# Gate and up of tokens 512 to 1023: from full products to seven block products with 256-token halves

## The chip, the cores and the metric

The kernel runs on one core of a Trainium2 chip. The metric is the device time of one execution in microseconds (us). The engines of a core work side by side, each through its own queue in order: TensorE (PE) multiplies matrices, VectorE (DVE), ScalarE (ACT) and GpSimd (POOL) do the elementwise work, SyncE (SP) issues the DMAs. PE writes its results into PSUM, from where VectorE and ScalarE take them.

## The reference

```python
x = A_x                                   # 1 x 2048 x 512, bfloat16
xn = layernorm(x)
qkv = xn @ wqkv                           # 512 x 1536; 32 heads of 16
pq, pk = q @ w_phi[h], k @ w_phi[h]       # 16 x 16 for each head
phi_q = concat(softmax(pq), softmax(-pq)) # 32 features; phi_k alike
kv, z = phi_k^T v, sum_s phi_k            # for each head, over all tokens
attn = (phi_q kv) / (phi_q z + 1e-6)
h = (xn @ w_gate) * (xn @ w_up)           # 512 x 1792 each
out = x + attn @ wo + h @ w_down          # 1792 x 512
```

All inputs and the output are bfloat16.

## The kernel before

2048 tokens are sixteen tiles of 128, in four groups of four (`GT` = 4, 512 tokens, `TT`). All weights and all of x stay in SBUF. `w_phi` is folded into the weights of q and k on the chip (`W1q`, `W1k`; steps `fq`, `fk`).

The work is cut into named steps, each a small function in the dictionary `steps`. One written list, `ORDER`, says in which order they are issued, and with `/v`, `/g` or `/a` on which engine (VectorE, GpSimd, ScalarE). No scheduler changes that order: every engine executes its own instructions in the order of the list, and semaphores hold it where data or a buffer is not ready. A second table, `SLOTS`, says which buffer of a ring each tile takes ("s" are six PSUM banks, "f" two more in the pool `ps_f`, "x", "g", "vt" are SBUF rings). The loop at the end also keeps "turns": after a VectorE step whose operands all lie in SBUF (its name matches `both_in_sbuf`), the next GpSimd instruction of the list waits for it.

The steps, by name:

- `s`, `sc`, `a`, `xt`: layer norm of a tile (statistics, scale, normalised x, DMA transposition). The transposed x of tokens 0 to 1023 lies in `xnT` (bfloat16), that of 1024 to 2047 in `x16` (float16).
- `k` or `vk`, `vc`, `kx`, `ky`, `kr`, `ki`, `kp`, `kv`: v and k products, exponentials on ScalarE, sums and reciprocals on VectorE, product on GpSimd, then the `kv` sums. `q`, `qx` to `qp`, `qt` are the same for q, with a DMA transposition; `ab`, `de`, `rd`, `ot`, `oT` are the attention of a tile.
- `g`, `gc`, `u`, `h` (`unit_steps`): gate and up of one group for 128 hidden columns: four matmuls for gate, a copy to SBUF (`gate_copy`), four matmuls for up, and the product of both on VectorE (`hidden`). Units 0 to 13 are tokens 0 to 511, units 14 to 27 tokens 512 to 1023; `half` issues the matmuls, with 512 columns.
- `p1` to `p7`, `k1` to `k3`, `j2`, `j7`, `j3`, `d4`, `m` (`block_steps`): gate (even block) and up (odd block) of tokens 1024 to 2047 by seven block products instead of eight. Tokens, input channels and hidden columns are each cut into two halves; `z` (sums of tokens) and `t` (differences of weights, after `up` has scaled them by a power of two) make the operands. A product is two matmuls with 512 columns into one of three PSUM banks `sa`, `sb`, `sc`. Bank `sa` keeps a running sum: product 1, copy `k1`, product 6 on top, copy `k2`, product 7, copy `k3`, product 4, then `d4`. The joins `j` add a bank and a kept copy; `m` multiplies up by gate.
- `f` (`fin_steps`): down product and attention output of one tile; `fs` adds x, `fo` stores.
- `n`, `wr`, `wf`, `wp`, `ws`, `inv`: powers of two for the scaled weights. `S`, `cb`, `ct`, `wt` and the steps with capital `P`, `K`, `A`, `J`, `X` (`pair_steps`): seven block products for the down product of six pairs of tiles of tokens 1024 to 2047.
- `=k`, `=ab`, `=f`, `=ab2`: change the PSUM pool of the two banks besides the six.

## Time and profile before

| | |
|---|---|
| time, median of 3 runs | 214.32 us (214.11 to 214.84) |
| the profiled execution | 214.6 us, span of its instructions 212.8 us |
| PE, DVE, ACT, POOL busy | 207.8, 181.5, 138.2, 140.3 us |
| instructions of these | 1368 matmuls, 333, 247, 133 |
| granted TensorE clock, mean | 0.999 |
| moved by DMA | 19.91 MB |

The profile is one execution, taken by the hardware profiler. A row of a group reads: line of the kernel, engine, operation, what it writes and reads, form, number of instructions, then busy time in us, mean length of one in ns, and the idle time of the engine ahead of them with what ended it. A row of the chain gives the start, the length, and the work. L333 is the matmul in `half`, L319 the one in `proj` (k, v, q), L797 the one in `block_steps`, L663 that in `fin_steps`, L924 that in `pair_steps`; L353 is `hidden`, L339 to L345 are the branches of `copy`, L819 is `times` (the m steps), L758 the weight differences, L894 the hidden sums, L507 the transposition of x.

### The profile page before, as it was taken

How to read it: one execution, taken by the hardware profiler on the slowest of the kernel's cores; microseconds unless marked ns; L12 is line 12 of the kernel's file. 1: busy time of each engine (PE TensorE's matmuls, PEld its weight loads, DVE VectorE, ACT ScalarE, POOL GpSimd, SP SyncE). 2: the span in 40 equal slices, each digit the busy share in tenths (PEclk: the TensorE clock that was granted, in tenths of full speed). 3: DMA queues.
4: the chain of work that ended last, by engine and by line, in shares of the span. 5: the costliest groups of instructions: out<-in, count | busy, mean ns of one | idle time of the engine just before them, and what ended most of it. 6: DMA issues, size and time to landing. Idle time of an engine off the chain costs nothing.

```text
span 212.8 us, 3868 instructions
## 1 busy us (share of the span) xinstructions
PE 207.8 (98%) x1368; PEld 109.8 (52%) x1368; DVE 181.5 (85%) x333; ACT 138.2 (65%) x247; POOL 140.3 (66%) x133
## 2 busy tenths in 40 slices
PE   7999999999999999999999999999999999999993
PEld 3554444444454455554454444444444455678982
DVE  4857998986967889889878999999999999997853
ACT  4616999977756897889943966765487457254200
POOL 3600350776678898987887986567697888927370
PEclk9999999999999999999999999999999999999999
DMA  5999996050133002021545540020405506525342
GB/s 161 260 283 385 376 288 80 12 115 0 28 78 72 0 3 49 0 52 37 101 89 88 111 99 18 11 43 6 99 0 93 84 2 138 87 42 91 74 117 74
DMA packets 47250, 19.91 MB, mean 94 GB/s; under 512 B 37504, under 2 KB 46976, under 8 KB 47104
## 3 DMA queue, kind: packets, MB, share of 16 engines
q1 hardware_dynamic: 47232, 19.69, 41.2%
q8 instruction: 10, 0.16, 0.3%
q14 instruction: 8, 0.07, 0.1%
HBM read 8.67 MB, written 2.10 MB: 51 GB/s over the span
## 4 chain that ended last, share of the span: by engine, by line
PE 91%; DMA 3%; DVE 2%; SPq 1%; issue 1%; DVEq 0%
PE fin L663 16%; PE g L333 12%; PE u L333 11%; PE sa L797 11%; PE k L319 6%; PE pv L319 6%; PE q L319 6%; PE sc L797 5%; PE da L924 4%; PE sb L797 3%; PE kv L574 2%; DMA oT<-otok 2%; PE db L924 2%; PE dd L924 2%; PE dc L924 2%; PE ab L611 2%
## 5 line engine op out<-in xcount | busy, mean ns | idle before, releaser
L533 DVE TENSOR_REDUCE sums<-e 128x64 f32<-128x1024 f32 x32 | 38.4, 1204 | 3.5 <-ACT e L521 3.3
L543 POOL TENSOR_TENSOR phiq<-e,rs 128x1024 bf16<-128x1024 f32 x16 | 31.0, 1944 | 11.4 <-ACT dK L341 4.2
L663 PE MATMUL fin<-wd,hT 128*128 128x512 bf16 (+2 forms) x154 | 37.9, 360 | 0.0
L543 POOL TENSOR_TENSOR phik<-e,rs 128x1024 bf16<-128x1024 f32 x16 | 30.9, 1940 | 7.3 <-DVE rs L538 2.8
L333 PEld LDWEIGHTS <-wgu 128*128 128x128 bf16 x240 | 22.8, 98 | 23.4 <-DMA wgu<-in_B_w_gate_dram 0.3
L333 PE MATMUL u<-xnT,wgu 128*128 128x512 bf16 (+1 forms) x120 | 27.9, 365 | 0.0
L333 PE MATMUL g<-xnT,wgu 128*128 128x512 bf16 (+1 forms) x120 | 27.8, 365 | 0.0
L353 DVE TENSOR_TENSOR hT<-u,g_sb 128x512 bf16<-128x512 f32 (+1 forms) x30 | 18.8, 637 | 5.5 <-PE u L333 5.4
L663 PEld LDWEIGHTS <-hT 128*128 128x128 bf16 (+1 forms) x154 | 14.5, 98 | 14.8
L262 POOL TENSOR_SCALAR ve<-mv 128x1 f32<-128x1 f32 (+1 forms) x7 | 2.1, 293 | 24.9 <-DVE mv L258 24.8
L538 DVE RECIPROCAL rs<-sums 128x64 f32<-128x64 f32 x32 | 17.2, 542 | 1.2
L521 ACT ACTIVATE e<-k 128x512 f32<-128x512 f32 x24 | 13.3, 598 | 6.8 <-PE k L319 6.7
L521 ACT ACTIVATE e<-q 128x512 f32<-128x512 f32 x24 | 13.5, 601 | 6.4 <-PE q L319 6.3
L797 PEld LDWEIGHTS <-T 128*128 128x128 f16 x112 | 10.6, 98 | 11.9
L797 PE MATMUL sa<-ss,T 128*128 128x512 f16 x56 | 16.2, 379 | 0.0
L339 ACT CAST g_sb<-g 128x512 bf16<-128x512 f32 (+1 forms) x21 | 11.4, 568 | 7.1 <-PE g L333 6.5
L341 ACT ACTIVATE k<-sa 128x512 f32<-128x512 f32 x19 | 11.3, 602 | 6.1 <-PE sa L797 6.1
L339 ACT COPY k<-sa 128x512 f32<-128x512 f32 x19 | 11.2, 589 | 5.8 <-PE sa L797 4.8
L698 ACT ACTIVATE junk<-wgu 128x1024 bf16<-128x1024 bf16 x14 | 14.8, 1059 | 0.0
L319 PEld LDWEIGHTS <-xnT 128*128 128x128 bf16 x96 | 9.0, 98 | 10.7 <-ACT xnT L307 1.4
L758 POOL TENSOR_TENSOR T<-wgu,T 128x512 f16<-128x512 bf16 x9 | 10.6, 1176 | 5.8 <-DVE T L758 3.9
L319 PEld LDWEIGHTS <-x 128*128 128x128 f16 x96 | 9.0, 98 | 10.1 <-DVE otok L639 0.2
(153 smaller groups left out, 480.2 us busy)
## 6 DMA issues: line engine op xcount, KB each, us to landing
out_dram<-o_sb SPq DMA_DIRECT2D x15, 128.0 KB, 2.0
wd<-in_B_w_down_dram SPq DMA_DIRECT2D x1, 1792.0 KB, 16.1
wgu<-in_B_w_gate_dram SPq DMA_DIRECT2D x2, 640.0 KB, 7.2
wgu<-in_B_w_up_dram SPq DMA_DIRECT2D x2, 640.0 KB, 8.3
xall<-in_A_x_dram SPq DMA_DIRECT2D x1, 1024.0 KB, 12.4
xall<-in_A_x_dram SPq DMA_DIRECT2D x4, 128.0 KB, 2.6
vk<-in_A_wqkv_dram SPq DMA_DIRECT2D x2, 256.0 KB, 3.7
wgu<-in_B_w_gate_dram SPq DMA_DIRECT2D x2, 256.0 KB, 4.7
```

The lines of the kernel that those rows point to most:

```text
L319: nc.tensor.matmul(ps, lhsT=xt(n)[:, j, :], rhs=w[:, j, :], start=(j == 0), stop=(j == DC - 1))
L333: nc.tensor.matmul(ps, lhsT=w[:, c, f * P:(f + 1) * P], rhs=xnT[:, c, T * TT + lo:T * TT + hi], start=(c == 0), stop=(c == DC - 1))
L339: A.copy(out=dst, in_=src)
L353: V.tensor_tensor(out=hT(T)[:, f, lo:hi], in0=ps, in1=g_sb[:, 0:hi - lo], op=ALU.mult)
L521: A.activation(out=held[s + "e", n][:, :, sign, :], in_=held[s, n].rearrange("p (g c) -> p g c", g=NG), func=AF.Exp, scale=(nrst if sign e ...
L533: V.tensor_reduce(out=sums[:], in_=ev(), axis=AX.X, op=ALU.add)
L538: V.reciprocal(out=rs[:].rearrange("p a b -> p (a b)"), in_=held.pop((s + "s", n))[:])
L543: eng.tensor_tensor(out=phi[:].rearrange("p g (x f) -> p (g x) f", f=DH), in0=ev(), in1=held.pop((s + "i", n))[:].to_broadcast((P, 2 * H, ...
L663: nc.tensor.matmul(held["fin", n, lo], lhsT=l, rhs=r, start=len(done) == 1, stop=len(done) == FC + DC)
L698: A.activation(out=out, in_=cols, func=AF.Square, accum_out=nrm[:, g, k:k + 1])
L797: nc.tensor.matmul(mine[bankname], lhsT=ww[:, j, :], rhs=xx[:, j, :], start=start and j == 0, stop=(j == hc - 1), skip_group_check=True)
L924: nc.tensor.matmul(mine[ps][:, 0:W], lhsT=l, rhs=r, start=bool(mine.pop((ps, "new"), False)), stop=True, skip_group_check=True)
```

## The change

Units 14 to 27 are taken away. Tokens 512 to 1023 get block steps of their own, with an N ahead of the name (`Np1.0`, `Nk1.0`, `Nj2.0`, ...), with halves of 256 tokens: a product is two matmuls with 256 columns, and keeps, joins and m steps work on 256 columns. The weight differences `t` are shared with tokens 1024 to 2047. The transposed x of these tokens moves from `xnT` to a tile of its own, `x4`, in float16, with token sums `s4` beside it (steps `Nz`). Since their gate and up are now scaled, their h is float16, and their denominators and output use the scale of the block products (`scale_of`). The banks `sa` and `sc` of the new blocks come from the two banks of `ps_f`, `sb` from the six; q and f steps no longer use `ps_f`. The tile of `t2` (differences of down weights) moves to smaller pieces in the "vt" ring, and the up results from "vt" to "g". `inv` is cut in two steps. The list and the slots are written anew: 1244 words instead of 1072.

The core of the diff (the list and the slot table are cut to a few lines):

```diff
 ORDER = """
-g2 gc2/v u0 g3 gc3/a u2 h2 g1 u1 gc1/v h1 fk2 g0 gc0/v u3 fka2/a h3 h0 fk0 fkv0/v g8 g4 fkv2/a fka0/a k0 gc8/v
...
+g3 gc3/a =k g1 gc1/a fk2 fk0 g0 u3 fkv2/v fkv0/v fka2/a fka0/a k1 ky1 kx1 u0 gc0/v h3 k0 u1 k2 h0 kr1 h1 ki1 kx0
+ky0 kr0 s6 s5 ky2 n1.0 g4 g6 gc4/a u6 g7 n0.5 kx2 gc6/a gc7/a s7 k3 kp1/g s4 sc4 kx3 n1.6 n0.6 ky3 u7 h7 h6 a5/g
+xt5 u4 g12 g11 g13 h4 ki0 u12 g9 u13 a6/g kp0/g gc11/a s9 s11 s10 s8 u11 a4/a xt4 n0.3 gc9/a kr2 gc13/a n0.1 h11
+h13 xt6 wq g10 gc10/a gc12/a kr3 n2.4 u9 h9 ki2 kv0 g5 sc8 a11/g a10/g vk5.0 a8/g xt11 ki3 vk5.1 kp2/g a9/a
...
+Np2.1 ab7 de7/a f3.6 p5.1 f3.7 k3.1/a rd7 ot7 qy13 p4.1 p3.0 =f fs3 Np1.1 up31/a Nk1.1/a Np1.0 Nk1.0/a p2.3
+Np6.1 qx13 j3.0 Np6.0 p2.2 Nj2.1 Nk2.1/a j7.1 d4.1 Nk2.0/a up30/a t11/g m2.1/g Np2.0 Nj2.0 t12/g p3.1 j3.1 Np7.0
+Np7.1 Nk3.1/a Nk3.0/a p1.2 k1.2/a p1.3 qr9 m7.1/g Np4.1 Np4.0 Nd4.0/a p5.2 t13/v Np5.0 up40/a Nd4.1 p6.2 Nj7.0
...
-    xnT = npool.tile([P, DC, HALF], BF16, name="xnT", tag="xnT")
+    xnT = npool.tile([P, DC, TT], BF16, name="xnT", tag="xnT")
+    x4 = xpool.tile([P, DC, TT], F16)
+    s4 = xpool.tile([P, 4, DC // 2, TT // 2], F16)
...
-        return xnT[:, :, n * P:(n + 1) * P] if n < QT else x16[:, :, (n - QT) * P:(n - QT + 1) * P]
+        x, lo = (xnT, 0) if n < GT else (x4, GT) if n < QT else (x16, QT)
+        return x[:, :, (n - lo) * P:(n - lo + 1) * P]
...
-    for u in range(2 * FC):
+    for u in range(FC):
         unit_steps(u)
...
-        new_bank = bank_f if n in QF else bank
+        new_bank = bank
...
-    def block_steps(b):
+    def block_steps(b, group):
         k, g = b // 2, b % 2
         hc = DC // 2
+        n = TT // 2 if group else TT
+        tag = "N" if group else ""
         cols = pair_cols(k)[:, g]
+        A11, A12, A21, A22 = narrow if group else wide
...
         def h(t, i):
-            return hT(NGRP // 2 + t)[:, k + i * FH, :]
+            return hT(1)[:, k + i * FH, t * n:(t + 1) * n] if group else hT(NGRP // 2 + t)[:, k + i * FH, :]
...
                 if start:
-                    mine[bankname] = bank(bankname)
+                    new_bank = bank_f if group and bankname != "sb" else bank
+                    mine[bankname] = new_bank(bankname)[:, 0:n]
...
-                mine[name] = ring(xnpool, "x", [P, TT], F32, name)
+                mine[name] = ring(xnpool, "x", [P, n], F32, name)
                 copy(eng, mine[name][:], mine["sa"], gate_scale if g == 0 else None)
...
-                    mine["u", i] = ring(vpool, "vt", [P, TT], BF16, "u_sb")
+                    mine["u", i] = ring(gpool, "g", [P, n], BF16, "u_sb")
                     V.tensor_tensor(out=mine["u", i][:], in0=mine[ps], in1=mine[kept][:], op=ALU.add)
...
     for b in range(2 * FH):
-        block_steps(b)
+        block_steps(b, 0)
+        block_steps(b, 1)
...
+    SMALL = ((0, 2), (2, 4), (4, 6), (6, FH))
...
-    QF = (8, 9, 13, 10, 14)
```

## The prediction

> **What bounds the kernel now.** I read the page's first part, then the chain of work that ended last, then busy time by stretch, and last the groups by form.

> ```profile
> PE 207.8 (98%) x1368; PEld 109.8 (52%) x1368; DVE 181.5 (85%) x333; ACT 138.2 (65%) x247; POOL 140.3 (66%) x133
> PEclk9999999999999999999999999999999999999999
> PE 91%; DMA 3%; DVE 2%; SPq 1%; issue 1%; DVEq 0%
> ```

> TensorE (PE) is busy 98% of the span, and the chain that ended last lies on it for 91%. A busy PE need not be PE at its peak, so I look at its pace in the chain, listed in order of time:

> ```profile
> 9.73 0.44 PE u L333 x4
> 22.30 1.73 PE g L333 x8
> 24.89 1.73 PE u L333 x8
> 170.50 0.86 PE sc L797 x4
> 204.11 1.53 PE dc L924 x14
> 208.48 0.78 PE da L924 x7
> 209.28 0.48 DVE o_sb L953
> ```

> Eight matmuls with 512 columns take 1.73 us, four take 0.86: 0.216 us each, in bfloat16 (g, u) as in float16 (sc). Fourteen with 256 columns take 1.53 us: 0.109 each, and the bfloat16 ones at the start (u x4) 0.44, or 0.11. At full clock these are flat paces, so PE is fed almost without a gap. After its last product only one join (0.48 us) and the last store are left. PE's work is the time, unless another engine falls behind. How near the others are:

> ```profile
> 0.00:20.00 20.00, 18.59 (x132) 9.69 (x133) 13.14 (x35) 9.07 (x21) 5.92 (x21) 1.00 0.93 264
> 20.00:100.00 80.00, 80.00 (x517) 38.66 (x516) 69.04 (x113) 67.28 (x120) 54.82 (x43) 1.00 0.37 83
> 100.00:177.00 77.00, 77.00 (x424) 36.34 (x423) 71.75 (x129) 51.39 (x88) 59.94 (x48) 1.00 0.33 62
> 130.00:190.00 60.00, 59.95 (x348) 30.28 (x347) 57.99 (x103) 36.26 (x60) 44.15 (x38) 1.00 0.29 53
> ```

> After the stretch's length the columns are PE, weight load, VectorE (DVE), ScalarE (ACT), GpSimd (POOL). From 100 to 177 us, where block products run, DVE is busy 71.75 of 77.0 us (93%), and from 130 to 190 us 58.0 of 60 (97%), with PE still full. DVE is the one engine with little left.

> **The change part by part.** The rows that price it:

> ```profile
> L333 PE MATMUL g<-xnT,wgu 128*128 128x512 bf16 x104 | 25.6, 379 | 0.0
> L333 PE MATMUL u<-xnT,wgu 128*128 128x512 bf16 x104 | 25.5, 379 | 0.0
> L924 PEld LDWEIGHTS <-wgu 128*128 128x128 f16 x84 | 8.1, 98 | 1.6
> L353 DVE TENSOR_TENSOR hT<-u,g_sb 128x512 bf16<-128x512 f32 x26 | 17.2, 670 | 5.0 <-PE u L333 5.0
> L353 DVE TENSOR_TENSOR hT<-u,g_sb 128x256 bf16<-128x256 f32 x4 | 1.7, 422 | 0.5 <-PE u L333 0.4
> L343 DVE CAST g_sb<-g 128x512 bf16<-128x512 f32 x7 | 4.8, 680 | 2.6 <-PE g L333 2.6
> L343 DVE CAST vt<-pv 128x512 bf16<-128x512 f32 x4 | 2.7, 672 | 0.1
> L339 ACT CAST g_sb<-g 128x512 bf16<-128x512 f32 x19 | 10.6, 588 | 7.0 <-PE g L333 6.5 <-DVE hT L353 0.4
> L339 ACT CAST g_sb<-g 128x256 bf16<-128x256 f32 x2 | 0.7, 373 | 0.1
> L341 ACT ACTIVATE k<-sa 128x512 f32<-128x512 f32 x19 | 11.3, 602 | 6.1 <-PE sa L797 6.1
> L341 ACT ACTIVATE dK<-da,inv 128x256 f32<-128x256 f32 x7 | 3.3, 470 | 6.8 <-issue 4.0 <-PE da L924 2.7
> L819 POOL TENSOR_TENSOR hT<-u_sb,hT 128x512 f16<-128x512 bf16 x7 | 8.0, 1156 | 2.2 <-DVE hT L819 1.4 <-DVE down L727 0.8
> L819 DVE TENSOR_TENSOR hT<-u_sb,hT 128x512 f16<-128x512 bf16 x14 | 7.9, 585 | 0.0
> L894 DVE TENSOR_TENSOR wgu<-hT 128x384 f16<-128x384 f16 x5 | 1.6, 327 | 0.0
> L758 DVE TENSOR_TENSOR T<-wgu 128x512 f16<-128x512 bf16 x5 | 2.5, 493 | 0.0
> L341 ACT ACTIVATE wgu<-wgu,up 128x1024 bf16<-128x1024 bf16 x12 | 13.9, 1155 | 0.0
> ```

> *PE.* Units 14 to 27 go: 14 x 8 = 112 matmuls of 512 columns, 112 x 0.216 = 24.2 us. Fourteen blocks of seven products of two matmuls come: 196 of 256 columns, 196 x 0.109 = 21.4 us. The weight load of one takes 98 ns and fits under 109. Projections and down products keep their number. Saved on the path: 2.8 us, and nothing else of PE changes.

> *DVE.* Gone are 14 `hidden` products (0.670), 7 wide and 1 narrow gate casts, 4 v casts (these go to ACT) and two wide keeps (taken at the casts' 0.68): 9.4 + 4.8 + 0.4 + 2.7 + 1.4 = 18.7 us. New are 42 half joins and 7 half `direct` products; no such row exists before, and I take the 256-column row, 0.422, for it too reads PSUM and writes 16 bits: 49 x 0.422 = 20.7. The other moves: 9 half m steps at some 0.35 (an estimate, over half of 0.585) and 4 wide ones fewer, +0.8; five hidden sums more (0.327) 1.6; two weight differences (0.493) 1.0; two wide copies from PSUM (0.68) 1.4; in all +5, and the rest is smaller than a step or two. So DVE goes from 181.5 to about 188.5, all of it beside PE as long as it keeps up. [...]

> *ACT.* 41 half keeps (between 0.373 and 0.470; I take 0.42), 7 half directs, 4 more wide keeps (0.60), 4 v casts and 2 more weight scalings (1.155) come, 7 gate casts (0.588) go: about +20 us, to 158 of some 210 (75%). *POOL* gets 12 half m steps and 4 wide ones (1.156): some +8 us, to about 148. Both stay covered by PE's 205, but neither cover is loose: ACT's list is densest before 120 us, where before it was already busy 67.3 of 80 us.

> *Where the list is tight.* Between the first block product and the step `=ab2` the new list holds 98 + 25 + 12 pairs of wide matmuls (products, down, q), 98 pairs of half ones and 4 attention steps: 58.3 + 21.4 + 1.0 = 80.7 us of PE. The DVE steps between the same two points sum to 87.8 us of durations. The same count of the old list gives 77.8, and that stretch is the one from 100 to 177 us, busy 71.75: neighbours overlap, a factor 0.92. So 0.92 x 87.8 = 81 us of DVE meet 81 us of PE: 100%, where before it was 93%, and 97% was sustained for 60 us without loss. Behind `=ab2` DVE has room (35 us of durations under 39 of PE), so steps can slip some us. I put the loss at 0.4 us; its ends are 0 (the 97% row) and 3 us (DVE's old idle share of 4% stays).

> *The start.* The first v and k products of tokens 512 on move up. Old and new:

> ```profile
> 11.72 1.03 PE L333 MATMUL g<-xnT,wgu 128*128 128x512 bf16 x4
> 43.11 0.38 PE L319 MATMUL pv<-vk,xnT 128*128 128x512 bf16 x1
> 27.53 6.43 SPq L507 DMA_TRANSPOSE xnT<-xn  x4
> DMA to landing us min/median/max: 3.7/5.5/6.0
> wT<-in_A_wqkv_dram SPq DMA_TRANSPOSE x2, 5.0
> ```

> The list starts at 11.72 us; ahead of `vk5.0` it now has 22 wide groups of 0.864, four half ones of 0.436, two folds and a `kv` (some 1 us): 21.7 us, so PE is there at 33.4 us instead of 43.1. The first transposed x was issued at 27.5 and takes 3.7 to 6.0: it lands at 31 to 33.5, the next ones some 1.2 us apart. The wait lies between 0 and 2 us; I take 0.2, as the transposition is listed about a microsecond earlier. On SP's queue the transposition of the q weights (`wq`) moves up from sixth to fourth, behind the third x; issued near 30.7 us it lands near 36, and `fq0`, which reads it, comes at 37.7 us. The turns make the next POOL step wait for a DVE step that works in SBUF alone; five more of these m steps at 0.585 us or less make at most 3 us of POOL waiting, in an engine that is idle for a third of the span, with only later feature products queued behind: nothing on the path, and at most those 3 us if that cover were gone.

> Sum for the profiled execution (214.6 us, of which 212.8 are span): 214.6 - 2.8 + 0.4 + 0.2 = 212.4. The median of the runs lies 0.3 below that execution (214.3), so the prediction is 212.1.

> **The rivals.** *VectorE takes over in the product stage.* If the halves cost as much as the 256-column joins at the end of the chain (0.48 instead of 0.422), DVE asks for 84 us against 81, and some of its idle time stays: 1 to 2.5 us lost, 213.1 to 214.6. For it: the 100% above. Against: 97% without loss, and slack behind `=ab2`.

> *The hand-offs of the small bank (ends slower).* A half block keeps its running sum in one bank `sa`: product 1, copy by ACT, product 6, copy, product 7, copy, product 4. PE may not go on until the copy is done. Counting list steps, old blocks leave at least 1.3 us of other PE work between two such products, for a copy of 0.60; new half blocks leave as little as 0.65 (mostly 0.9 to 1.1) for a copy of 0.37 to 0.47, and the ACT queue may have a weight scaling of 1.155 us in front. There are 42 such hand-offs, each on PE's in-order queue; from 2.8 / 42 = 0.067 us each on the gain is gone. At 0.1 to 0.2 us each it costs 4.2 to 8.4 us: 215.7 to 219.9, middle 217.5. For it: the thin spacing and the denser ACT. Against: the old list has the same kind of hand-off 42 times, and PE's pace shows none.

> *Half-width matmuls are not half price.* If weight load and start cost kept one at 0.123 us (24.2 / 196) or more, the gain is gone; at 0.14 it is 196 x 0.031 = 6.1 us dearer, 218.2. [...] The chain's 0.216 and 0.109 speak plainly against it.

> **How the numbers follow.** The forecast (PE sets the time, up to 1 us lost; 211.4 to 212.9) gets 0.57. VectorE's takeover 0.22: 0.12 of it faster, 0.08 no change, 0.02 slower. Hand-offs 0.14, half-width price 0.03, both slower. An early start that waits its full 2 us and more 0.04, half faster and half no change. About 0.3% (0.64 us) is what the measurement can tell from no change. So faster 0.57 + 0.12 + 0.02 = 0.71, the same 0.08 + 0.02 = 0.10, slower 0.19. The range starts at 211.2 (no loss anywhere and the run spread of 0.2) and reaches to 216.0, where it takes in the takeover and the cheap end of the hand-offs; some 0.15 is left above.

> **What would show it.** Right: the new half products in the chain at 0.109 us, chain shares on PE of 90% or more, DVE near 188 and over 95% in the product stage, ACT near 158, the first v product near 33.5 us, and the last join near 207.1. Wrong: gaps of PE ahead of `sa` that ACT's keep ends (hand-offs), PE waiting for banks that a DVE join frees (takeover), a wait of the first v product for the transposition, or a half product above 0.11 us.

## The result, and the profile after

The changed kernel takes 214.12 us (median of 22 runs, 212.70 to 215.21), the kernel before, measured beside it, 214.80 us (22 runs, 214.11 to 215.63). The ratio is 0.9968, 95% interval 0.9952 to 0.9983: faster by 0.7 us. Forecast were 2.2 us less. The profiled execution took 215.05 us, 0.9 more than the median, so its waits are probably larger than those of a usual execution.

The page's first part, granted clock and chain of the changed kernel:

```profile
PE 206.5 (97%) x1452; PEld 117.8 (55%) x1452; DVE 185.3 (87%) x372; ACT 153.2 (72%) x296; POOL 149.8 (70%) x146
PEclk9999999999999999999999999999999999999999
PE 78%; DMA 9%; DVE 6%; SPq 2%; ACT 1%; POOL 1%; issue 1%; DVEq 0%; ACTq 0%; POOLq 0%
```

PE held 91% of the chain before and holds 78% now; DMA came to 9%, VectorE to 6%. So the time is no longer PE's work alone. The stretches (columns as in the prediction: length, then PE, weight load, DVE, ACT, POOL) say where:

```profile
20.00:100.00 80.00, 77.59 (x549) 37.76 (x548) 72.75 (x125) 73.83 (x136) 65.43 (x51) 1.00 0.55 117
100.00:177.00 77.00, 76.96 (x471) 44.48 (x470) 72.29 (x158) 55.20 (x115) 59.31 (x58) 1.00 0.16 28
130.00:190.00 60.00, 60.00 (x398) 34.76 (x396) 54.41 (x120) 33.72 (x68) 42.37 (x39) 1.00 0.29 59
```

From 100 to 190 us, where the new half products run, PE is full (76.96 of 77, 60.00 of 60). All that is lost lies between 20 and 100 us: 80.00 - 77.59 = 2.4 us idle, where before there was none. PE's rows in order of time show five waits in it:

```profile
33.60 0.38 PE L337 MATMUL pv<-vk,x 128*128 128x512 bf16 x1
38.34 0.41 PE L471 MATMUL pq<-bd,wT 64*128 64x64 bf16 x16 [0.26 <-DMA wT<-in_A_wqkv_dram]
43.51 0.39 PE L337 MATMUL pv<-vk,x 128*128 128x512 bf16 x1 [0.85 <-DMA x<-xn]
72.54 0.43 PE L590 MATMUL kv<-vt,phik 128*128 128x68 bf16 x8 [0.39 <-POOL phik L559]
74.43 0.43 PE L590 MATMUL kv<-vt,phik 128*128 128x68 bf16 x8 [0.17 <-POOL phik L559]
94.24 0.61 PE L678 MATMUL fin<-wo,oT 128*128 128x512 bf16 x2 [0.72 <-DMA oT<-otok]
```

The brackets sum to 2.39 us, all of the 2.41. (By starts it is 3.2 us: each first matmul also starts late by what the modelled end of its neighbour covers, 0.16 us.) (L337, L590, L627, L678 and L824 are the matmuls of `proj`, `kv`, `ab`, `fin_steps` and `block_steps` in the changed file, L960 that of `pair_steps`, L471 that of the folds.) In steps these are `fq0` at 38.34, `vk7` at 43.51, `kv14` and `kv15`, and `f3.8`. The first v product, at 33.60, did not wait. What each waited for, out of the chain of waits:

```profile
31.84 6.46 DMA wT<-in_A_wqkv_dram
40.98 2.47 DMA x<-xn
66.50 2.10 DVE ss L796
72.15 2.23 POOL phik L559 x2
89.45 4.74 DMA oT<-otok
```

and SP's queue in order of time:

```profile
31.84 2.92 SPq L491 DMA_TRANSPOSE wT<-in_A_wqkv_dram  x1
34.85 7.36 SPq L523 DMA_TRANSPOSE x<-xn  x5
```

The q weights took 6.46 us to land; the x of `vk7` was issued only at 40.98, fifth in a row on SP's queue; VectorE's token sum `z0` (line 796) took 2.10 us, which made GpSimd's phik late; the transposed attention output of tile 3 landed after 4.74 us.

### The profile page after: what moved, and what is told of

It reads as the page before. It is cut to its first block, busy times and chain, and to the rows that moved or that the text cites. A ratio compares the mean times of both kernels' runs of the same rounds, so it can differ in the third digit from the quotient of the medians.

```text
span 213.3 us, 4174 instructions
## 1 busy us (share of the span) xinstructions
PE 206.5 (97%) x1452; PEld 117.8 (55%) x1452; DVE 185.3 (87%) x372; ACT 153.2 (72%) x296; POOL 149.8 (70%) x146
## 4 chain that ended last, share of the span: by engine, by line
PE 78%; DMA 9%; DVE 6%; SPq 2%; ACT 1%; POOL 1%; issue 1%; DVEq 0%; ACTq 0%; POOLq 0%
PE sa L824 16%; PE fin L678 15%; PE sc L824 9%; PE k L337 5%; PE q L337 5%; PE da L960 5%; PE pv L337 4%; PE sb L824 4%; DMA wT<-in_A_wqkv_dram 3%; PE u L351 3%; DMA wgu<-in_B_w_up_dram 2%; PE g L351 2%; DMA oT<-otok 2%; PE db L960 2%; PE dd L960 2%; PE dc L960 2%
## 5 line engine op out<-in xcount | busy, mean ns | idle before, releaser
L678 PE MATMUL fin<-wd,hT 128*128 128x512 bf16 (+2 forms) x154 | 37.1, 359 | 0.0
L559 POOL TENSOR_TENSOR phiq<-e,rs 128x1024 bf16<-128x1024 f32 x16 | 31.5, 1975 | 4.8 <-DVE hT L846 2.7
L824 PEld LDWEIGHTS <-T 128*128 128x128 f16 x224 | 21.9, 98 | 17.4 <-issue 0.5
L846 POOL TENSOR_TENSOR hT<-u_sb,hT 128x256 f16<-128x256 bf16 (+1 forms) x23 | 21.1, 920 | 5.3 <-DVE T L774 3.0
L357 ACT COPY k<-sa 128x512 f32<-128x512 f32 (+1 forms) x42 | 19.5, 483 | 5.6 <-PE sa L824 4.1
L359 ACT ACTIVATE k<-sa 128x512 f32<-128x512 f32 (+1 forms) x41 | 19.7, 494 | 4.9 <-PE sa L824 4.2
L824 PEld LDWEIGHTS <-wgu 128*128 128x128 bf16 x168 | 16.3, 98 | 12.3
L337 PEld LDWEIGHTS <-x 128*128 128x128 f16 x144 | 13.4, 98 | 14.4 <-DMA x<-xn 1.1
L678 PEld LDWEIGHTS <-hT 128*128 128x128 f16 (+1 forms) x154 | 14.0, 98 | 11.8
L337 PE MATMUL pv<-vk,x 128*128 128x512 bf16 x48 | 18.2, 379 | 0.8 <-DMA x<-xn 0.8
L337 PE MATMUL k<-vk,x 128*128 128x512 bf16 x48 | 18.2, 379 | 0.0
L824 PE MATMUL sa<-ss,T 128*128 128x512 f16 x56 | 16.3, 379 | 0.0
L839 DVE SCALAR_TENSOR_TENSOR hT<-sc,k 128x512 f16<-128x512 f32 (+1 forms) x28 | 15.3, 548 | 1.1 <-PE sc L824 0.9
L359 ACT ACTIVATE wgu<-wgu,up 128x1024 bf16<-128x1024 bf16 x14 | 16.0, 1152 | 0.0
L843 DVE TENSOR_TENSOR u_sb<-sc,k 128x512 bf16<-128x512 f32 (+1 forms) x28 | 15.0, 545 | 0.6 <-PE sc L824 0.5
L537 ACT ACTIVATE e<-q 128x512 f32<-128x512 f32 x24 | 13.9, 601 | 1.9 <-POOL phik L559 1.4
L351 PE MATMUL u<-xnT,wgu 128*128 128x512 bf16 (+1 forms) x64 | 14.6, 352 | 0.1
```

The source lines that it names most:

```text
L337: nc.tensor.matmul(ps, lhsT=xt(n)[:, j, :], rhs=w[:, j, :], start=(j == 0), stop=(j == DC - 1))
L351: nc.tensor.matmul(ps, lhsT=w[:, c, f * P:(f + 1) * P], rhs=xnT[:, c, lo:hi], start=(c == 0), stop=(c == DC - 1))
L357: A.copy(out=dst, in_=src)
L359: A.activation(out=dst, in_=src, func=AF.Identity, scale=scale)
L559: eng.tensor_tensor(out=phi[:].rearrange("p g (x f) -> p (g x) f", f=DH), in0=ev(), in1=held.pop((s + "i", n))[:].to_broadcast((P, 2 * H, ...
L678: nc.tensor.matmul(held["fin", n, lo], lhsT=l, rhs=r, start=len(done) == 1, stop=len(done) == FC + DC)
```

## Experiments

Theory at this point: PE's own saving came, and was given back in these five waits, which have three causes: the start, the sum z0 (one of the token sums `z`, VectorE's row at 66.50), and the late transposition of tile 3 (oT3). The rival: VectorE or GpSimd is short of time from 20 to 100 us in any order, so that a wait taken away comes back at the next step. Each ratio below is to the kernel before.

**The start and the sum z0, each alone.** Both edits move words of the list and nothing else. The first:

```diff
-... vk6.0 s14 fq0 xt10 s15 s12 sc12 xt8 xt9 xt7 ky4 kx4 ky5 fqa0/v vk6.1 ky6 kv1 g2 ...
+... vk6.0 s14 xt7 xt10 s15 s12 sc12 xt8 xt9 ky4 kx4 ky5 vk6.1 ky6 kv1 fq0 fqa0/v g2 ...
```

> The changed kernel with two steps moved in its list: the transposition of x of token tile 7 (xt7) is issued ahead of those of tiles 10, 8 and 9, and the fold of the q weights (fq0) comes after the next v and k products and a kv step, 1.1 us later on PE. Waits theory (the new waits of PE in the first half gave the gain back): the waits of 0.43 us ahead of fq0 and 1.0 us ahead of vk7 go, the time falls by 1.0 to 1.4 us against the changed kernel, ratio to the kernel before 0.990 to 0.993. Backlog theory (VectorE and ScalarE are so full that a wait taken away here comes back later): under 0.4 us, ratio 0.995 to 0.998. Chance theory (the waits of the profiled execution were its own): about half, 0.5 to 0.8 us, ratio 0.993 to 0.995.

Measured: 213.82 us, ratio to before 0.9938 [0.9915, 0.9961]. The waits at `fq0` and `vk7` are gone, the others stand (0.39 us at `kv14`, 0.69 us at `f3.8`). The second:

```diff
-... kp12/g kp13/g z0/v n0.2 kx14 ... kvm0 kvm1 =ab ...
+... kp12/g kp13/g n0.2 kx14 ... kvm0 kvm1 z0/v =ab ...
```

> The changed kernel with one VectorE step moved: the token sum z0, which took 2.10 us while GpSimd worked (0.90 in the kernel before), is issued after kvm1 instead of ahead of the features of tiles 14 and 15. Waits theory: the features are ready 2 us earlier, the waits of 0.56 and 0.33 us ahead of kv14 and kv15 go, the time falls by 0.7 to 1.0 us, ratio 0.992 to 0.994. Backlog theory: the 2.1 us of VectorE stay in its queue and delay the next joins or attention steps instead; under 0.3 us, ratio 0.996 to 0.999. If z0 takes 0.9 us at its new place, its length was due to what GpSimd did beside it; if it takes 2.1 again, it is slow wherever GpSimd runs.

Measured: 213.54 us, 0.9934 [0.9912, 0.9956]. At its new place z0 took 0.82 us. `kv14` and `kv15` no longer wait; `vk7` still does (0.88 us), and a new wait stands at 97 us (0.74 us, an attention product for a transposed phiq). Two causes, then, worth 0.6 and 0.7 us of the median by the middles of the intervals (0.9968 to 0.9938 and to 0.9934). Each interval still overlaps that of the change a little; and `fq0` and `f3.8` did not wait in the second profile, which its edit does not explain.

**The last wait, and all three.** `f3.8` is moved from behind `oT3` to just ahead of `f3.6`, some 4 us later; then all three moves together:

```diff
-... k3.0/a oT3 f3.8 fs0 rd6 ... ab7 de7/a f3.6 ...
+... k3.0/a oT3 fs0 rd6 ... ab7 de7/a f3.8 f3.6 ...
```

> The changed kernel with one PE step moved: the down product's attention part f3.8, which was listed right behind the transposition of its operand oT3 and waited 0.88 us for it, comes some 6 us of PE work later. Waits theory: 0.5 to 0.9 us less, ratio 0.993 to 0.995. Backlog theory: PE's products then stand 0.9 us earlier against the joins, and PE waits there instead; under 0.3 us, ratio 0.996 to 0.998. Chance theory: the transposition took 4.7 us in that one execution against a usual 2.5, so 0.0 to 0.3 us on the median, too.

> The three edits together (xt7 and fq0, z0, f3.8). Waits theory: 2.5 to 3.2 us less than the changed kernel, so the whole saving of 2.8 us on PE against the kernel before shows, ratio 0.983 to 0.988, and PE waits for nothing longer than 0.3 us between 15 and 205 us. Backlog theory: VectorE, at 185 of 213 us before, would have to be busy some 98% from 60 to 177 us, and PE waits for its joins; under 1 us less, ratio 0.992 to 0.997. Hand-off theory (PE waits for ScalarE's copies of the small bank once it runs ahead): waits of 0.1 us or more at many of the 42 half hand-offs, ratio 0.990 to 0.995.

Measured: alone 214.71 us, 0.9988 [0.9967, 1.0008], no gain; all three 212.97 us, 0.9905 [0.9889, 0.9922], short of the 0.983 to 0.988 expected. The wait for oT3 only went to the next in line: with `f3.8` moved alone the attention product behind it waits 0.43 us for VectorE's otok (the attention output before its transposition). That profile also shows how much the waits change between executions: its start is that of the change, yet `fq0` does not wait and `vk7` only 0.20 us. PE with all three moves:

```profile
75.36 1.02 PE L337 MATMUL q<-W1q,x 128*128 128x512 bf16 x4 [0.20 <-DVE fro L728]
93.28 0.41 PE L627 MATMUL ab<-KV,phiqT 128*128 128x68 bf16 x8 [1.28 <-DVE otok L654]
```

The attention product at 93.28 waits for VectorE's otok, which waits for a buffer that oT3 still reads: its transposition took 4.59 us, from 87.76 to 92.35. Moving the reader does not help while the transposition is late. Start and z0 without the third move:

> The change with two of the three moves at once: the transposition xt7 ahead of its four neighbours and the first product of the fq0 group behind kv1, and the VectorE sum z0 behind kvm1. Waits theory: the two savings of the single runs add, about 0.65 and 0.75 us of the median behind the change itself, so a ratio near 0.990 against the kernel before (about 212.7 us), unless the attention chain of tiles 4 to 7 takes some of it back with a wait of 0.5 to 1.5 us near 90 to 97 us (then 0.992). Rival, that the single gains were chance of the chip or one and the same slack: ratio 0.9935, no better than either alone. Against the run of all three moves (0.9905) it says what moving f3.8 is worth on top: nothing, if its wait only goes to the next in line.

Measured: 212.67 us, 0.9892 [0.9872, 0.9913]. The two add, the third move shows no gain on top, and the late oT3 costs 1.37 us of idle at `f3.8` in the profiled execution (the slowest of its six).

**Why transpositions land late.** The trace also records the packets of two other DMA queues, marked "instruction": 16 KB ones on q8 every 14 to 23 us, 8 KB ones on q14. Which of them falls on which transfer is called the placement below. The view of DMA queues (packets, MB, time as a share of 16 engines; then issues with the median us to landing), changed kernel, 88 to 92 us:

```profile
q1 hardware_dynamic: 2104, 0.52, 96.1%
q14 instruction: 1, 0.01, 2.8%
q8 instruction: 1, 0.02, 2.2%
oT<-otok SPq DMA_TRANSPOSE x2, 3.6
phiqT<-phiq SPq DMA_TRANSPOSE x1, 4.9
```

Both instruction packets of the stretch start (90.67 and 91.45 us) within the two late transpositions. If q8 carries TensorE's own instructions, more of them ahead move it. The next kernel is the change with one line altered: as many warm-up columns at the head (3588 for 3584), cut into 32 more products.

```diff
-    warm_up(7)
+    warm_up(39, 92)
```

> The change with its seven warm-up products of 512 columns at the head replaced by 39 of 92 columns: the same columns, 32 more TensorE products, so 64 more TensorE instructions ahead of everything. Nothing else differs. Theory, the transpositions that land late (4.9 and 4.7 us in place of 3.1 and 2.4) are held up by the 16 KB packets of the instruction queue, which come every 250 or so TensorE instructions: those packets come 3 to 5 us earlier in the whole program (90.7 goes to about 86, 36.1 to about 31.5, 50.8 to about 47), and the late transpositions are other ones: those issued 83 to 86 us, while the oT transposition that f3.8 waits for lands in about 2.5 us, and its wait of 0.9 us goes. The x transpositions issued 26 to 31 us then meet the packet, and the first product may start up to 1 us later. Time: ratio between 0.994 and 1.000, by which of the two weighs more. Rival, the late transpositions come from their own queue (13 transpositions in 21 us, one behind another): the same two are late again by the same 2 us, whatever the packets do, and the time is that of the change (0.997).

Measured: 212.84 us, 0.9893 [0.9869, 0.9917], better than expected. The times of the 16 KB packets, and from issue to landing the transpositions on them (from the trace's packets and DMA rows):

```
            16 KB packets (q8), the first seven       phiqT, oT around 82-84   phiqT, oT3 around 88-90
change      17.2 36.1 50.8 68.6 90.7 108.0 127.7      82.76: 3.15  84.09: 2.45   88.11: 4.94  89.45: 4.74
+64         13.5 33.1 46.9 64.1 82.9 101.0 121.4      81.72: 4.55  83.06: 3.67   88.22: 3.62  89.57: 2.77
            8 KB packets (q14)
change      28.4 33.7 57.0 91.4 96.1 100.0 141.3 142.6 192.6 200.6
+64         28.4 33.3 56.9 90.7 93.5  98.2 139.8 140.6 190.6 198.8
```

The 16 KB packets came 3 to 8 us earlier with TensorE's count, q14's by at most 2.6 us in a program that had itself become faster; the late pair is now the one at 82 us, which has slack, and `f3.8` starts only 0.11 us late. The same shift changed VectorE's z0, by a chain of its own. VectorE's, then GpSimd's rows, first of the change, then of the shifted kernel:

```profile
66.50 2.10 DVE L796 TENSOR_TENSOR ss<-x 128x1024 f16<-128x1024 f16 x1
64.22 3.83 POOL L559 TENSOR_TENSOR phik<-e,rs 128x1024 bf16<-128x1024 f32 x2
```

```profile
66.44 0.69 DVE L796 TENSOR_TENSOR ss<-x 128x1024 f16<-128x1024 f16 x1
64.16 1.94 POOL L559 TENSOR_TENSOR phik<-e,rs 128x1024 bf16<-128x1024 f32 x1
66.81 2.12 POOL L559 TENSOR_TENSOR phik<-e,rs 128x1024 bf16<-128x1024 f32 x1 [0.71 <-DMA phiqT<-phiq]
```

In the change the second phik product ran until 68.05, and z0 ended 0.55 us after it, as if it had stood until GpSimd was done. The other profiles bear this out. In all fourteen, 19 such sums of 1024 columns on VectorE started under a running GpSimd product; each ended 0.55 us after that product, whatever its own length came to (0.82 to 2.10 us). The five that started while GpSimd stood idle took 0.63 to 0.69 us. In the shifted kernel a packet (64.1 us) held the phiqT transposition issued at 62.10 us until 66.65, GpSimd paused for it, and z0, started in that pause, took 0.69. So the waits of `kv14` and `kv15` went too, which I had not expected. That the running product holds the sum is read from the ends alone, 0.55 us behind it every time; what holds it the trace doesn't show.

**z0 on GpSimd.**

```diff
-... kp13/g z0/v n0.2 ...
+... kp13/g z0/g n0.2 ...
```

> The change with one word altered: z0 stays at its place and goes to GpSimd instead of VectorE. Theory A, VectorE was held by GpSimd (its sum of two 16-bit operands waits until the GpSimd product in flight has ended): on VectorE no operation of the stretch 64 to 69 us is long any more, rs for the phik of kv14 comes about 1.4 us earlier, GpSimd takes about 2.1 us for z0 itself between 68 and 70.2 us, where it stood idle for 2.5 us, and the waits of kv14 and kv15 shrink from 0.9 to under 0.4 us: ratio about 0.995 (0.5 us less than the change alone). Theory B, the 2.10 us are the work of z0 itself at that place: VectorE is freed in the same way, so the waits shrink too; the two differ in what GpSimd shows, since the second half of the same sum (73.8 us, 1.16 us on VectorE beside a GpSimd product) then stays long by A and shortens by B only if its place moves. Rival, GpSimd is the bound there: kv14 waits 0.5 us more, ratio 0.999 or more.

Measured: 213.71 us, 0.9934 [0.9913, 0.9955]. GpSimd ran z0 from 67.65 (2.13 us) and its next phik at 69.74 instead of 70.55; of the `kv` waits 0.17 us of idle is left. The gain is a little above what was expected; in this profile `fq0` and `f3.8` did not wait either, so not all of it is z0's. The next such sum, z2, left on VectorE, took 2.03 us there: it started 1.48 us ahead of the end of a GpSimd product.

**Moves and shift combined.**

> All three moves and the 64 further TensorE instructions at the head. With the packet theory the wait of 1.45 us that was left at 93 us (VectorE's otok behind an oT transposition of 4.6 us) falls to under 0.5 us, and the time goes to about 0.986 to 0.989 of before, near the 2.8 us that TensorE's own work became shorter; if the x transpositions at 27 to 33 us are hit in its place, about 0.990. With the queue theory the wait stays above 1 us and the ratio at 0.9905.

> The change with two edits: the move of the start (xt7 ahead of its four neighbours, the fq0 product behind kv1) and the 64 further TensorE instructions at the head. Placement theory: the shift took away the waits of kv14, kv15 and f3.8 (1.8 us) and left those of fq0 and vk7 (1.7 us together in its profile); the move takes those two. The gains add, ratio 0.983 to 0.987 (about 211.5 to 212.2 us), with TensorE waiting under 1 us in all between 23 and 105 us, and the time is then before less the 2.8 us of its shorter products, or a little under. Rival, that each gain is only taken back by the next wait in line: 0.989 as with the shift alone.

> The change with the move of the start, z0 on GpSimd at its place, and the 64 further TensorE instructions. With z0 on GpSimd VectorE can't be held at 66 us whatever the placement, so nothing is left but a wait of about 0.3 us at kv15: ratio 0.983 to 0.987, equal to the same without the move of z0 within 0.002, since there the shift alone had freed z0. Rival, GpSimd's 2.1 us more make it late for the fro chain or the phiq products at 76 to 84 us, where it has under 1 us to spare: 0.989 or more, with a new TensorE wait of 0.5 us or more between 72 and 90 us.

Measured: all three moves and the shift 213.17 us, 0.9917 [0.9893, 0.9941], no better than the moves alone: the wait at 93 us fell to 0.42 us of idle as the packet theory has it, but z0 behind `kvm1` now made VectorE late for `fro`, a sum for the scaled weights (0.66), and a packet at 83.4 us made an attention product wait for phiqT (0.53). Start and shift: 212.20 us, 0.9872 [0.9839, 0.9904], the lowest median tried, though the interval overlaps those of 0.9892 and 0.9893. Its page and stretch, of the fastest of its six executions (211.89 us):

```profile
PE 92%; DMA 3%; DVE 1%; SPq 1%; issue 0%; ACT 0%
20.00:100.00 80.00, 79.95 (x569) 39.89 (x567) 74.58 (x131) 76.90 (x142) 68.44 (x54) 1.00 0.59 117
```

PE is full again from 20 to 100 us (79.95 of 80) and holds 92% of the chain, with VectorE, ScalarE and GpSimd at least as busy there as in the change: the rival, too little time in any order, fails here. With z0 on GpSimd as well: 213.62 us, 0.9929 [0.9900, 0.9958]. In that order the rival held for GpSimd; it pays for the late phiqT and for z0:

```profile
65.82 1.94 POOL L559 TENSOR_TENSOR phik<-e,rs 128x1024 bf16<-128x1024 f32 x1 [0.73 <-DMA phiqT<-phiq]
67.71 2.13 POOL L796 TENSOR_TENSOR ss<-x 128x1024 f16<-128x1024 f16 x1
69.80 4.27 POOL L559 TENSOR_TENSOR phik<-e,rs 128x1024 bf16<-128x1024 f32 x2
```

and `kv14` and `kv15` wait 0.71 and 0.62 us for it. The move that gained in one placement lost in the other.

**The control, and twice the shift.** The kernel before with the same one-line shift, and the change with 71 products of 50 columns.

> The control: the kernel before, with its seven warm-up products of 512 columns replaced by 39 of 92, so that the packets of the instruction queue fall 64 TensorE instructions earlier; its block products are as before. If the shift is worth something of its own (a warmer head, another start), before gains as the change did, ratio near 0.992. If the shift only moves the packets off the places where the change has no slack, before, whose attention transpositions are spread over more time and wait nowhere, does not change: 0.998 to 1.002. A loss of up to 0.5% would say that before stood in a lucky place.

> The change with 71 warm-up products of 50 columns in place of seven of 512: 64 more TensorE products, 128 more instructions, twice the shift. The packet that stood at 90.7 us comes at about 78 to 80 us, and the one after it at about 96 to 98; the packet of 36.1 us at about 27 to 29, within the first x transpositions. Placement theory: which wait appears follows the packets. The transpositions that lie on a packet land 1 to 2 us late, and those issued 86 to 90 us land in about 3.1 and 2.5 us, so that f3.8 does not wait; ratio 0.989 to 0.997 by what is hit in their place, the first x transpositions above all. Rival, the shift by 64 gained for another reason, as the head's: the same 0.989 here with the same waits.

Measured: before with the shift 216.25 us, 1.0058 [1.0033, 1.0083]; the change with twice the shift 215.95 us, 1.0057 [1.0027, 1.0086]. Both lose. PE of the shifted kernel before, the DMA queues around its last transposition (204.5 to 209 us), and the same queues of the kernel before itself (203 to 206 us):

```profile
114.47 0.61 PE L663 MATMUL fin<-wo,oT 128*128 128x512 bf16 x2 [0.57 <-DMA oT<-otok]
208.79 0.61 PE L924 MATMUL dc<-wo,oT 128*128 128x256 bf16 x4 [0.63 <-DMA oT<-otok]
```

```profile
q1 hardware_dynamic: 1233, 0.53, 71.6%
q8 instruction: 1, 0.02, 1.5%
...
oT<-otok SPq DMA_TRANSPOSE x1, 3.8
```

```profile
q1 hardware_dynamic: 923, 0.38, 46.9%
...
oT<-otok SPq DMA_TRANSPOSE x1, 2.4
```

A packet on the last transposition (3.8 instead of 2.4 us) costs right at the end, where nothing can cover it; another costs at 114 us. (Some 0.8 us more of this execution is a wait for weights at 9 to 10 us, which I can't tie to a packet; the execution was 0.9 us above its median.) So the shift has no gain of its own, and the kernel before stood in a good place. With the shift in both kernels, the change is about 1.6% faster (0.9893 to 1.0058, two ratios to the same unshifted kernel), of which that wait for weights may be a part; with it in neither, 0.3%. In the change with twice the shift `f3.8` does not wait, as expected, but `kv14` and `kv15` do again, and a packet sits at 205.2 us on the last transposition (4.51 us), which PE's end waits for. The waits of its profiled execution (these three and two short ones of v products, at 33.9 and 42.7 us) come to 3.0 us by starts, against 2.8 saved, which fits its 215.25 us; why its median lies 0.7 us above that, with runs up to 217.78, is open.

## Why the prediction was wrong

The size was wrong, the direction right: 2.2 us less were forecast, 0.7 came. What failed is the term for PE's waits: the sum had 0.6 us of them (0.4 in the product stage, 0.2 at the start), the profiled execution has 2.4 us of idle, 3.2 by starts, and none of it behind 100 us, where the products are densest. By its steps:

- **PE's own work: right.** The new half products (the first row is four of them) run at 0.109 us, the down products likewise, as the chain after shows:

```profile
100.75 0.44 PE sa L824 x4
196.76 1.53 PE da L960 x14
210.15 0.48 DVE o_sb L989
```

  That last join was forecast near 207.1 us. It comes 3 us later, which is what the waits cost beyond the 0.6 us allowed for them, within half a microsecond. The version without waits comes to 0.9872 [0.9839, 0.9904], or 2.75 us of 214.92 under before, against 2.8 reckoned from 112 and 196 matmuls.
- **The product stage: over-priced.** VectorE was to be at 100% with 0.4 us lost; it is busy 72.29 of 77 us and PE loses 0.04. (The stage starts at 88.4 us; the wait of `f3.8` at 94.24 lies in it, but a transposition ended that one, not VectorE.) The half joins cost what the 256-column row said:

```profile
L843 DVE TENSOR_TENSOR u_sb<-sc,k 128x256 bf16<-128x256 f32 x14 | 5.8, 416 | 0.6 <-PE sc L824 0.5
L839 DVE SCALAR_TENSOR_TENSOR hT<-sc,k 128x256 f16<-128x256 f32 x14 | 5.8, 413 | 1.0 <-PE sc L824 0.9
L357 ACT COPY k<-sa 128x256 f32<-128x256 f32 x21 | 7.9, 377 | 3.7 <-PE sa L824 2.3 <-DVE hT L839 1.1
```

  0.416 and 0.413 against 0.422 taken. VectorE ended at 185.3, ScalarE at 153.2, GpSimd at 149.8 us (forecast 188.5, 158, 148). The items listed for ScalarE add up to 23 us and not to the 20 that were forecast, and 15 were measured (a half keep takes 0.377 to 0.385 us, 0.42 was taken); neither engine set the time by its sum.
- **The start: mis-sized, 0.2 us taken, 1.1 us of idle measured** (0.26 at `fq0`, 0.85 at `vk7`). I followed the first x product, which was right to 0.1 us (33.5 forecast, 33.60), and the q weights only to an estimated landing of 36 us; they were issued 1.1 us later than I took (31.84) and took 6.46 us, with instruction packets at 33.7 and 36.1 us in their flight. The x of `vk7`, fifth of five in SP's queue, I did not follow at all. Taking both out gained about 0.6 us of the median.
- **GpSimd "nothing on the path": wrong.** I priced the turns as waits of GpSimd for VectorE and missed the other direction, VectorE's sum beside a running GpSimd product: z0 ended 0.55 us after the product and took 2.10 us instead of 0.69. It cost 0.56 us of idle at `kv14` and `kv15`; moving z0 gained about 0.7 us of the median.
- **The attention of the first eight tiles: not in the sum.** The change brings thirteen of SP's transpositions of phiq and otok (the third to the fifteenth) into the 21 us from 76.7 to 97.7; before, the same places of the queue took 32 us, from 99.0 to 131.3. I did not list SP's queue there. That alone delays nothing by 2 us (an undisturbed oT lands in 2.4); with an instruction packet on top it cost 0.72 us at `f3.8`.
- **The rivals.** Hand-offs of bank `sa`: refuted, with PE at 60.00 of 60. VectorE's takeover: refuted, by the same rows. Half-width matmuls above half price: refuted, at 0.109; no run shows the 0.123 us or more that it supposed. The early start was the nearest, with a chance of 0.04 and the wrong product. None named the placement of the instruction packets, which is worth as much as the change: the kernel before gave 1 and 1.0058 in two placements, the change 0.9968, 0.9893 and 1.0057 in three. (The ranges of the rivals start from two bases, 211.5 and 212.1 us; no refutation hangs on it.) The change itself adds 84 matmuls and their 84 weight loads (1452 against 1368 of each), and its list is written anew, so its later packets fall elsewhere.

## What to carry to other kernels

When an edit moves work earlier, follow every transfer that it makes earlier through its queue, with the issue time and the place in line of the last one and not only of the first. Where one engine's instruction ends only behind another engine's, as VectorE's sum did here 0.55 us behind GpSimd's product, look at both orders. And when a tuned kernel changes by under 1%, time it in two or three placements (a few more instructions at the head) before calling the edit good or bad: here the same edit, held against one and the same kernel before, measured 0.3% faster, 1.1% faster and 0.6% slower. Place the kernel before in the same ways, too: with one shift in both, this edit came out about 1.6% faster.
